# An FFN stage of two batches pulled ahead of its second half, and three more transposes given to the DMA

## The chip, the cores and the metric

The kernel runs on one core of a Trainium2 chip. The metric is the time of one execution on the device in microseconds (us). A run counts as slow when it is more than 1.5% above the fastest run of the same kernel; comparisons use the fast runs alone. A wait of TensorE is given as the profile has it, as the idle time ahead of a product.

## The reference

Eight batches of 448 tokens go through attention with a squared ReLU in place of the softmax (12 heads of width 64), and its output goes through one feed-forward block (768 to 3072 to 768) with a layer norm without offset ahead of it.

```python
scores = scale * np.matmul(q, k.transpose(0, 1, 3, 2))      # 8 x 12 x 448 x 448
attn = np.maximum(scores, 0.0) ** 2 / S
x = np.matmul(attn, v)                                      # then 8 x 448 x 768
# ...
xn = (x - mu) / np.sqrt(var + 1e-06) * g_ln
ch = np.maximum(xn @ w_ch1, 0.0) @ w_ch2
return (x + ch).astype(np.float32)
```

## The kernel before: the parts that matter

Heads are handled in pairs, six pairs to a batch: pairs 0 to 5 are batch 0, 6 to 11 batch 1, 12 to 17 batch 2. Attention of batch 0 runs by itself (to 28 us). From then on TensorE works in three layers. FFN1 of a batch makes 24 tiles of the hidden layer `h`. Between those tiles stand bursts ("excursions") of three tiles of attention scores, for the next batch. FFN2 follows: two tiles of batch 0 with plain products (`ffn_2_first`), everything else two tiles at a time with seven half-size products instead of eight (`seven`), for which VectorE makes sums of quarters of the second weight, `w2`, and of `h`.

All of the loads from memory that concern us are issued by GpSimd, one after another, in the order of the program. The transposes of `x_tok` (the residual by token) and of q and k are DMA transposes issued by SyncE. Pairs 0 to 11 get their q and k transposed on TensorE; pairs from 12 on by a DMA transpose out of a ring of three places.

```python
PE_T = 2                                   # batches whose q/k are transposed on TensorE

def att_T(i, copy=None, bank=None):
    if i >= PE_T * NPAIR:                  # pairs from 12 on
        new_qkT(i)
        nc.sync.dma_start_transpose(qkT[i], qk_ring[:, i % 3].rearrange("p j c -> p (j c)"))
        return
    # ... 16 transposes on TensorE and a copy out of PSUM

def load_qk(i):
    # ... q, k and the last keys of one pair of heads into the ring: three loads by GpSimd
    nc.gpsimd.dma_start(q_to, q[b, heads].rearrange("x (p j) d -> p j x d", j=NJ))
    nc.gpsimd.dma_start(k_to[:, :NF], k[b, heads, :SF].rearrange("x (p t) d -> p t x d", t=NF))
    nc.gpsimd.dma_start(k_to[:SS, NF], k[b, 2 * a:2 * a + 2, SF:].rearrange("x s d -> s x d"))

def w2_sums(slot, a, b, op, part):
    r = slice(part * KH // 2, (part + 1) * KH // 2)
    nc.vector.tensor_tensor(w2[:, slot, r], w2[:, a, r], w2[:, b, r], op=op)

IN_FIRST = (5, 8, 11, 14, 17, 20)          # FFN1 tiles of batch 0 followed by a burst
T_IN_FIRST = {10: 3, 13: 4, 16: 5}         # pairs 9, 10, 11 transposed on TensorE after these tiles
X_AT = (9, 10, 11, 12, 13, 14)             # DMA transposes of x_tok
STATS_AT = {0: (18, 21, 23), ...}          # layer norm statistics on VectorE

# ... the main sequence
        load_heads(1, [("q", 0, 2), ("k", 0, 2), ("k last", 0, H)])
        load_heads(1, [("q", 2, 4), ("k", 2, 4)])
        load_w1(0)
        load_w1(1)
        load_w1(2)
        load_heads(1, [("q", 6, 6), ("k", 6, 6), ("v", 0, H), ("v last", 0, H)])
        for c in range(3, NCH):
            load_w1(c)
        # ... attention of batch 0
        load_w2(B11, 0, 0)
        load_w2(B21, 1, 0)
        load_w2(B12, 0, 1)
        load_w2(B22, 1, 1)
        nc.gpsimd.memset(qk_ring, 0.0)
        i = PE_T * NPAIR
        load_qk(i)
        load_qk(i + 1)
        load_qk(i + 2)
        load_v(i)
        for b in range(B):
            ffn_1_all(b)
            if b == 0:
                ffn_2_first()              # two tiles of batch 0, plain
            else:
                ffn_2_all(b)               # the rest, seven products for two tiles
```

Of the kernel before, what the change touches and what calls it, by code (L numbers as in the profile page):

```python
# [11 lines left out]
def kernel(  # L12
# [93 lines left out]
    nc.vector.memset(v1_sb[:, H * NF * D:], 0.0)  # L106

# [18 lines left out]
    PE_T = 2  # L126
    EARLY = H * NJ * D
# [113 lines left out]
    def q_of(i, r):  # L241
        if i < PE_T * NPAIR:
            return by_j(flat(i)[r, :S])
        return qkT[i][r, :NJ, :SP]

    def k_of(i, r, t, keys):
        c0 = (S if i < PE_T * NPAIR else NJ * P) + t * P
        return flat(i)[r, c0:c0 + keys]

    def att_T(i, copy=None, bank=None):  # L250
        if i >= PE_T * NPAIR:
            new_qkT(i)
            nc.sync.dma_start_transpose(qkT[i], qk_ring[:, i % 3].rearrange("p j c -> p (j c)"))
            return
        new_qkT(i)
        if i == 0:
            for t, cp, n in ((0, nc.vector.tensor_copy, S), (1, nc.scalar.copy, SF)):
                ps = bf_view(next_f())
                pe_T(0, t, ps, range(NJ - t))
                cp(flat(0)[:, t * S:t * S + n], ps[:, :n])  # L260
            return
        if bank is None:
            bank = next_f() if i <= NPAIR else next_spare()
        ps = bf_view(bank)
        pe_T(i, 0, ps)
        pe_T(i, 1, ps, range(NJ - (i == 1)), S)
        n = S + (SF if i == 1 else S)
        (copy or nc.vector.tensor_copy)(flat(i)[:, :n], ps[:, :n])  # L268
# [108 lines left out]
    def gain(b, ki):  # L377
        nc.scalar.activation(xc[:, ki, :], xT_of(b, ki), Act.Identity, scale=g_sb[:, ki:ki + 1])

    def center(b):  # L380

        mean_ps = spare[1][:, :S]

        def parts(k0, k1):
            for ki in range(k0, k1):
                center_part(ki, mean_ps)

        def first():
            for c in range(2):
                nc.tensor.matmul(mean_ps[c * D:(c + 1) * D, :], ones[:, :D], xs, start=True, stop=True)  # L390
            parts(0, 2)

        return [first, lambda: parts(2, 4), lambda: parts(4, 6)]

    def center_part(ki, mean_ps):
        nc.vector.scalar_tensor_tensor(xc[:, ki, :], mean_ps, g_sb[:, ki:ki + 1], xc[:, ki, :],  # L396
# [16 lines left out]
    def ffn_rstd(b):  # L413
        ts = tiles_of(b)
        r = rstd[:, ts[0]:ts[-1] + 1]
        nc.scalar.activation(r, mv_sb[:, ts[0]:ts[-1] + 1, 1], Act.Sqrt, bias=eps_sb)
# [8 lines left out]
    def ffn_1(ni, bank=None):  # L425
        ps = (next_f() if bank is None else bank)[:, :S]
        for ki in range(K1):
            for c in range(2):
                n0 = ni * P + c * D
                nc.tensor.matmul(ps[c * D:(c + 1) * D, :], w1[:, ki, n0:n0 + D], xc[:, ki, :],  # L430
                                 start=(ki == 0), stop=(ki == K1 - 1))
        nc.scalar.activation(h[:, ni, CARRY:], ps, Act.Relu)  # L432

    def h_cols(b, m):
        c0 = CARRY + m * P - b * S
# [34 lines left out]
    held_stores = []  # L470

    def plain_part(b, m, dh, part, parts, box):
        if part == 0:
            box[m] = next_f()[:, :HD]
        n = K2 // parts
        cols = h_cols(b, m)
        for ki in range(part * n, (part + 1) * n):
            slot = ((B11, B12), (B21, B22))[ki // KH][dh]
            for c in range(2):
                t0 = cols.start + c * D  # L480
                nc.tensor.matmul(box[m][c * D:(c + 1) * D, :], h[:, ki, t0:t0 + D],  # L481
                                 w2[:, slot, ki % KH, :], start=(ki == 0), stop=(ki == K2 - 1))
        if part == parts - 1:
            o_t = new_acc() if dh else new_o()
            scaled_plus(o_t, box[m], m, x_half(m, dh))
            held_stores.append(lambda: store(o_t, m, dh * HD, (dh + 1) * HD))
# [21 lines left out]

    def seven(b, pair, banks, last, between):

        m1, m2 = 2 * pair, 2 * pair + 1
        a11, a12 = (h[:, r, h_cols(b, m1)] for r in (slice(0, KH), slice(KH, K2)))
        a21, a22 = (h[:, r, h_cols(b, m2)] for r in (slice(0, KH), slice(KH, K2)))
# [95 lines left out]
    def queued(i):  # L609
        if PE_T * NPAIR <= i + 3 < NP_ALL:  # L610
# [100 lines left out]
    def ffn_1_first():  # L711
        f_ps, m_ps = next_f(), next_f()
        tiles = [t[:, :S] for t in (f_ps, m_ps, spare[1], next_sc()[:, 0])]
        for ki in range(K1):
            if ki < GAIN_FIRST:
                center_part(ki, mean0)
# [3 lines left out]
            for ni, ps in enumerate(tiles):  # L720
                nc.tensor.matmul(ps, w1[:, ki, ni * P:(ni + 1) * P], xc[:, ki, :],  # L721
                                 start=(ki == 0), stop=(ki == K1 - 1))
        for ni, ps in enumerate(tiles):
            nc.scalar.activation(h[:, ni, CARRY:], ps, Act.Relu)
        for t in range(2):
            att_square(NPAIR, t)
        excursion(1)
# [3 lines left out]
    IN_FIRST = (5, 8, 11, 14, 17, 20)  # L731
    T_IN_FIRST = {10: 3, 13: 4, 16: 5}
    X_AT = (9, 10, 11, 12, 13, 14)
    V_AT = {21: PE_T * NPAIR + 2, 23: PE_T * NPAIR + 4}
    STATS_AT = {0: (18, 21, 23), 1: (10, 16, 19, 22), 2: (2, 5, 8, 14)}
    IN_SECOND = (3, 6, 9, 13, 15, 18, 21)
    IN_REST = (1, 4, 7, 10, 13, 16, 19)

    def ffn_1_all(b):
        ms = tiles_of(b)  # L740
        for ni in range(NI0 if b == 0 else 0, K2):
            if b == 0 and ni == NI0:
                ffn_1_first()
            if b == 0 and ni == X_AT[0]:

                nc.sync.dma_start(held, h[:1, ni - 1, CARRY:CARRY + 16])
            if b == 0 and ni in X_AT:
                ffn_x(b, X_AT.index(ni))
            if b == 0 and ni in V_AT:
                load_v(V_AT[ni])  # L750
            bursts = (IN_FIRST, IN_SECOND, IN_REST)[min(b, 2)]
            ffn_1(ni, spare[1] if b < B - 1 and ni in bursts and len(ready) > 1 else None)
            flush()
            at = STATS_AT[min(b, 2)][:len(ms)]
            if ni in at:
                ffn_stats(ms[at.index(ni)])
            if b == 1 and ni in SUMS_AT:
                w2_sums(*LATE_SUMS[SUMS_AT.index(ni)])
            if b == 0:
                if ni in IN_FIRST:  # L760
                    excursion(3)
                if ni == IN_FIRST[-1] + 3:
                    next_AV(bank=spare[1])
                if ni in T_IN_FIRST:
                    att_T(NPAIR + T_IN_FIRST[ni])
            elif b < B - 1:
                if ni in bursts:
                    excursion(3, **(dict(third=(nc.scalar, nc.vector), evac_by=nc.scalar) if b == 1 else {}))
                    while ni > bursts[1] and held_stores:
                        held_stores.pop(0)()  # L770
                if ni == min(bursts[-1] + 3, K2 - 1):
                    flush_loads()
                    next_AV(bank=spare[1])

    CENTER_AT = (4, 6, 8)
    SUMS_AT = (0, 1, 2, 4, 7, 11)
    LATE_SUMS = [(o, x, y, op, part)
                 for o, x, y, op in ((B_BOT, B21, B22, Alu.add), (B12, B12, B22, Alu.subtract),
                                     (B21, B21, B11, Alu.subtract)) for part in range(2)]
    def ffn_2_first():  # L780
        b = 0
        ffn_rstd(b)
        box = {}
        assert not ready
        steps = center(1)
        n = 0
        for dh in range(2):

            order = [(m, part) for m in range(2) for part in range(4)]
            if dh:  # L790
                order.sort(key=lambda x: x[1] // 2)
            for m, part in order:
                plain_part(b, m, dh, part, 4, box)
                if n < K1 - 1:
                    gain(1, n)
                if n == 3:
                    gain(1, K1 - 1)
                if n in CENTER_AT:
                    steps[CENTER_AT.index(n)]()
                if n == 2:  # L800
                    for ki in range(K1):
                        ffn_x(1, ki)
                if n == 8:
                    carry(b)
                if n in (9, 10):
                    w2_sums(B_TOP, B11, B12, Alu.add, n - 9)
                if n in (13, 15):
                    w2_sums(B_SUM, B11, B22, Alu.add, (n - 13) // 2)
                n += 1

    def ffn_2_all(b):
        ffn_rstd(b)
        x_bank, y_bank = f_turn.items
        z_bank = spare[0]
        first = b * S // (2 * P)
        pairs = range(first, (b + 1) * S // (2 * P))
# [7 lines left out]
        def between(n):  # L824
            n += 7 * (pr - first)
            if n == (8 if len(pairs) == 2 else 1):
                carry(b)
                if b < B - 1:
# [14 lines left out]
    with tc.manual_schedule(engines=set(ENGINES)):  # L843
# [3 lines left out]
        load_heads(1, [("q", 0, 2), ("k", 0, 2), ("k last", 0, H)])  # L847
        load_heads(1, [("q", 2, 4), ("k", 2, 4)])
        load_w1(0)
        load_w1(1)  # L850
        load_w1(2)
        load_heads(1, [("q", 6, 6), ("k", 6, 6), ("v", 0, H), ("v last", 0, H)])
# [8 lines left out]
        load_w2(B11, 0, 0)  # L861
        load_w2(B21, 1, 0)
        load_w2(B12, 0, 1)
        load_w2(B22, 1, 1)
        nc.gpsimd.memset(qk_ring, 0.0)
        i = PE_T * NPAIR
        load_qk(i)
        load_qk(i + 1)
        load_qk(i + 2)
        load_v(i)  # L870
        for b in range(B):
            ffn_1_all(b)
            if b == 0:
                ffn_2_first()
            else:
# [32 lines left out]
```

## Time and profile before

| | before |
|---|---|
| time, median of the first 3 runs | 520.9 us (519.87 to 521.59) |
| profiled span, granted clock | 518.9 us, 0.999 |
| TensorE busy | 511.8 us, 99% |
| VectorE, ScalarE, GpSimd busy | 71%, 53%, 43% |

Parts 1 and 2 of the profile's page. In part 2 the span is cut in 40 slices of 13 us; a digit is the busy share in tenths, PEclk the TensorE clock that was granted, and the row DMA the mean busy share of the 16 DMA engines.

```profile
span 518.9 us, 13591 instructions
...
PE 511.8 (99%) x5689; PEld 306.5 (59%) x5689; DVE 370.4 (71%) x658; ACT 276.8 (53%) x456; POOL 222.6 (43%) x255
...
PE   8999999999999999999999999999999999999996
...
PEclk9999999999999999999999999999999999999999
DMA  9999999999446992469934699269934300240022
GB/s 137 192 196 201 186 203 162 161 177 104 79 105 91 117 88 72 113 79 117 88 72 101 79 122 141 66 82 115 87 71 100 62 1 2 75 113 1 1 59 65
```

TensorE is at nine tenths or more in every slice but the ends, and the clock never drops. The DMA engines are at nine tenths or more in the first ten slices: they bring in the weights and the first inputs there. So TensorE sets the time, and the DMA engines have little slack before about 130 us.

The list of what TensorE waited for (engine and line, what it waited for, then us in total, times, longest us):

```profile
PE f L599 <- DVE w L103: 1.2, 1, 1.2
PE sc L288 <- DMA qkT_t<-qk_ring: 0.8, 1, 0.8
PE f L229 <- DMA w<-in_k_dram: 0.4, 1, 0.4
```

The whole kernel has 2.6 us of such waits. The chain of work that ended last, by engine, says the same:

```profile
PE 91%; DVE 3%; DMA 2%; ACT 2%; POOL 0%; issue 0%; POOLq 0%; ACTq 0%
```

The next lines are TensorE's timeline around 45 to 51 us: start, duration, line, product, and in square brackets (where there is one) the idle time ahead and what ended it. L430 is FFN1 and L229 the sixteen TensorE transposes of one pair.

```profile
46.27 0.76 PE L323 MATMUL f<-at,s_sb 128*64 128x448 bf16 x6
46.87 2.44 PE L430 MATMUL f<-xc,w 128*64 128x448 bf16 x24
49.14 0.68 PE L229 MATMUL f<-identity,w 112*64 112x112 bf16 x16
49.75 1.33 PE L430 MATMUL f<-xc,w 128*64 128x448 bf16 x12
51.01 0.55 PE L293 MATMUL sc<-qkT_t 64*128 64x448 bf16 x4
```

No line here has a bracket: FFN1 goes from tile to tile, and a pair's transposes add 0.61 us (from the start of L229 to that of the next line). The load of w1's fourth chunk, which tile 12 is the first to need, landed at 43.85. GpSimd's timeline has the issue of that load:

```profile
33.48 0.87 POOL L202 DMA_DIRECT2D w<-in_moe_w_ch_dram  x1 [3.39 <-DMA w<-in_moe_w_ch_dram]
```

The DMA engines of the same kernel from 36 to 56 us, in 40 slices of 0.5 us:

```profile
DMA  9999999999999999999999999999999999959999
GB/s 194 191 188 166 180 188 234 191 199 207 219 199 211 203 207 211 205 205 200 197 195 193 196 196 198 201 188 200 193 199 196 219 180 167 55 81 186 194 191 188
```

They keep close to 200 GB/s until about 52 us.

### The profile page before, as it was taken

To read this page: it belongs to the slowest core of one execution; us is meant where nothing else is said; L and a number is where in the kernel's file an instruction comes from. 1 tells how busy PE (TensorE), PEld (TensorE's weight loads), DVE (VectorE), ACT (ScalarE), POOL (GpSimd) and SP (SyncE) were. 2 spreads that over 40 slices of the span, in tenths; PEclk is the share of its full clock that TensorE was granted. 3 is DMA by queue.
4 is the path that set the end of the run, shared out by engine and by line. 5 is a ranking of instruction groups with operands and counts; after the bars stand their busy time and mean duration, and the time that the engine had idled before them with its cause. 6 is when DMAs were issued, how large, how long until landed. Compare 5 with 4: busy or idle time off the path is not lost.

```text
span 518.9 us, 13591 instructions
## 1 busy us (share of the span) xinstructions
PE 511.8 (99%) x5689; PEld 306.5 (59%) x5689; DVE 370.4 (71%) x658; ACT 276.8 (53%) x456; POOL 222.6 (43%) x255
## 2 busy tenths in 40 slices
PE   8999999999999999999999999999999999999996
PEld 4455566546765566655666556555665556665665
DVE  5966879778958669587685868787695866950255
ACT  6986633776247652476524765476524765234320
POOL 8727115778423853238532376247532000320031
PEclk9999999999999999999999999999999999999999
DMA  9999999999446992469934699269934300240022
GB/s 137 192 196 201 186 203 162 161 177 104 79 105 91 117 88 72 113 79 117 88 72 101 79 122 141 66 82 115 87 71 100 62 1 2 75 113 1 1 59 65
DMA packets 175245, 53.01 MB, mean 102 GB/s; under 512 B 154192, under 2 KB 175184, under 8 KB 175184
## 3 DMA queue, kind: packets, MB, share of 16 engines
q0 software_dynamic: 103680, 25.75, 53.0%
q1 hardware_dynamic: 70976, 26.03, 27.0%
q8 instruction: 44, 0.72, 0.6%
q10 hardware_dynamic: 528, 0.37, 0.2%
q14 instruction: 17, 0.14, 0.1%
HBM read 51.91 MB, written 11.01 MB: 121 GB/s over the span
## 4 chain that ended last, share of the span: by engine, by line
PE 91%; DVE 3%; DMA 2%; ACT 2%; POOL 0%; issue 0%; POOLq 0%; ACTq 0%
PE f L430 40%; PE f L498 34%; PE f L323 5%; PE sc L293 4%; PE f L481 3%; PE f L293 2%; DVE at L306 1%; ACT at L303 1%; DMA qkT_t<-qk_ring 1%; PE sc L288 1%; DMA w<-in_k_dram 1%; PE f L346 1%; PE f L721 1%; DVE xT L362 1%; DVE qkT_t L268 0%; ACT h L432 0%
## 5 line engine op out<-in xcount | busy, mean ns | idle before, releaser
L430 PE MATMUL f<-xc,w 128*64 128x448 bf16 x2256 | 225.5, 353 | 0.1
L430 PEld LDWEIGHTS <-w 128*64 128x64 bf16 x2256 | 125.9, 110 | 91.6 <-issue 13.6
L432 ACT ACTIVATE h<-f 128x448 bf16<-128x448 f32 x188 | 102.8, 547 | 102.5 <-PE f L430 97.6
L498 PE MATMUL f<-w,s_sb 128*64 128x384 bf16 (+2 forms) x1584 | 130.0, 324 | 0.0
L498 PEld LDWEIGHTS <-s_sb 128*64 128x64 bf16 x1584 | 90.0, 110 | 37.2
L303 ACT ACTIVATE at<-sc 128x896 bf16<-128x896 f32 x120 | 102.8, 918 | 5.1 <-PE sc L293 4.2
L306 DVE TENSOR_TENSOR at<-at 128x896 bf16<-128x896 bf16 x168 | 95.6, 618 | 4.9 <-ACT at L303 4.7
L531 POOL TENSOR_TENSOR o_t<-o_t,x_tok 128x384 f32<-128x384 f32 x26 | 24.4, 938 | 148.7 <-ACT o_t L530 148.7
L169 POOL DMA_DIRECT2D qk_ring<-in_q_dram x36 | 46.7, 1298 | 87.3 <-DMA qkT_t<-qk_ring 61.7
L299 DVE TENSOR_SCALAR at<-f 128x448 bf16<-128x448 f32 x89 | 52.7, 619 | 30.7 <-PE f L293 30.7
L530 ACT ACTIVATE o_t<-f,rstd 128x384 f32<-128x384 f32 x26 | 15.1, 582 | 93.5 <-issue 30.9
L492 DVE TENSOR_TENSOR s_sb<-h 128x1536 bf16<-128x1536 bf16 x65 | 64.1, 1002 | 0.0
L170 POOL DMA_DIRECT2D qk_ring<-in_k_dram x36 | 55.8, 1549 | 10.7 <-DMA w<-in_moe_w_ch_dram 10.7
L498 PE MATMUL f<-w,h 128*64 128x384 bf16 x624 | 52.9, 326 | 0.0
L171 POOL DMA_DIRECT2D qk_ring<-in_k_dram x36 | 46.8, 1300 | 5.1 <-DMA w<-in_moe_w_ch_dram 4.9
L498 PEld LDWEIGHTS <-h 128*64 128x64 bf16 x624 | 35.7, 110 | 15.3
L531 POOL TENSOR_TENSOR acc_t<-acc_t,x_tok 128x384 f32<-128x384 f32 x24 | 28.9, 1211 | 22.3 <-ACT acc_t L530 19.6
L323 PE MATMUL f<-at,v_ring 128*64 128x448 bf16 x288 | 35.7, 356 | 0.0
L181 POOL DMA_DIRECT2D v_ring<-in_v_dram x36 | 33.2, 1232 | 1.1 <-DMA qk_ring<-in_q_dram 1.1
L396 DVE SCALAR_TENSOR_TENSOR xc<-f,g_sb,xc 128x448 bf16<-128x448 f32 x45 | 28.5, 678 | 4.6 <-PE f L390 4.6
L362 DVE TENSOR_SCALAR xT<-f 128x448 bf16<-128x448 f32 x33 | 20.3, 617 | 15.5 <-PE f L323 12.5
L293 PE MATMUL sc<-qkT_t 64*128 64x448 bf16 x192 | 30.0, 356 | 0.1
(86 smaller groups left out, 391.0 us busy)
## 6 DMA issues: line engine op xcount, KB each, us to landing
w<-in_moe_w_ch_dram POOLq DMA_DIRECT2D x6, 768.0 KB, 12.9
w<-in_moe_w_ch_dram POOLq DMA_DIRECT2D x4, 1152.0 KB, 29.1
v_ring<-in_v_dram POOLq DMA_DIRECT2D x21, 192.0 KB, 4.9
qk_ring<-in_q_dram POOLq DMA_DIRECT2D x36, 112.0 KB, 5.2
qk_ring<-in_k_dram POOLq DMA_DIRECT2D x36, 96.0 KB, 5.3
out_dram<-o_t SPq DMA_DIRECT2D x8, 168.0 KB, 2.2
out_dram<-acc_t SPq DMA_DIRECT2D x7, 168.0 KB, 2.2
out_dram<-o_t SPq DMA_DIRECT2D x8, 144.0 KB, 2.1
```

The source lines that it names most:

```text
L170: nc.gpsimd.dma_start(k_to[:, :NF], k[b, heads, :SF].rearrange("x (p t) d -> p t x d", t=NF))
L171: nc.gpsimd.dma_start(k_to[:SS, NF], k[b, 2 * a:2 * a + 2, SF:].rearrange("x s d -> s x d"))
L293: nc.tensor.matmul(by_j(half[hh]), k_of(i, r, t, P), q_of(i, r), start=True, stop=True)
L299: nc.vector.tensor_scalar(at[:, x], half[x], 0.0, None, op0=Alu.max)
L303: nc.scalar.activation(at, ps[:, :, :S], Act.Relu)
L306: nc.vector.tensor_mul(attn[i, t], attn[i, t], attn[i, t])
L323: nc.tensor.matmul(ps[hh * D:(hh + 1) * D, :], weights, values, start=start, stop=stop)
L430: nc.tensor.matmul(ps[c * D:(c + 1) * D, :], w1[:, ki, n0:n0 + D], xc[:, ki, :], start=(ki == 0), stop=(ki == K1 - 1))
L432: nc.scalar.activation(h[:, ni, CARRY:], ps, Act.Relu)
L492: nc.vector.tensor_tensor(s_sb[:, n], x, y, op=op)
L498: nc.tensor.matmul(ps[c * D:(c + 1) * D, :d1 - d0], stat[:, ki, c * D:(c + 1) * D], w2[:, slot, ki, d0:d1], start=(start and ki == 0), sto ...
L531: nc.gpsimd.tensor_tensor(o_t, o_t, x_half(m, dh), op=Alu.add)
```

## The change

The change makes FFN1 of batches 0 and 1 one after the other, before any FFN2. w2 is then not needed until both are made, and its loads can keep out of the way of w1's. `h` has no room for all the tokens of two batches; the 256 tokens that are left over (tiles 5 and 6 of 128, in batch 1) lie in idle places, the rows of w2's unfinished sums and the scratch of the sums of `h`. w2's loads are issued later, at tile 22 of batch 0 and tile 5 of batch 1. The plain pair is now made of tiles 5 and 6, after FFN1 of batch 1. And pairs 9, 10 and 11 get q and k by DMA transpose, which spares TensorE 48 transposes but takes three more sets of small loads into the first 40 us. The sums of w2 move with its loads, four of them into FFN1 of batch 1.

```diff
+    nc.vector.memset(qk_ring, 0.0)
+    xc_1 = sums_flat[:, :K1 * S].rearrange("p (k s) -> p k s", k=K1)   # FFN1's input of batch 1
+    def h_extra(ki):                       # where the tokens of batch 1 lie that h has no room for
+        if ki < NXS:
+            return x_flat[:, ki * XP:(ki + 1) * XP]
+        # ...
+    DMA_T = NPAIR + 3
     def att_T(i, copy=None, bank=None):
-        if i >= PE_T * NPAIR:
+        if i >= DMA_T:
@@ FFN1's ReLU out of PSUM
+        elif b == 1:
+            nc.scalar.activation(h[:, ni, S:], ps[:, :HW - S], Act.Relu)
+            nc.scalar.activation(h_extra(ni), ps[:, HW - S:], Act.Relu)
@@ the places of things in FFN1
-    IN_FIRST = (5, 8, 11, 14, 17, 20)
-    T_IN_FIRST = {10: 3, 13: 4, 16: 5}
-    STATS_AT = {0: (18, 21, 23), 1: (10, 16, 19, 22), 2: (2, 5, 8, 14)}
+    BURSTS = {0: (5, 8, 11, 14, 17, 19), 1: (4, 7, 10, 13, 16, 19, 22), 2: (1, 4, 7, 10, 13, 16, 19)}
+    STATS_AT = {0: {18: 0, 21: 1, 23: 2}, 1: {8: 5, 11: 6}, 2: {11: 7, 14: 8, 17: 9}}
+    W2_AT = {(0, 22): ((B11, 0, 0), (B12, 0, 1)), (1, 5): ((B22, 1, 1), (B21, 1, 0))}
+    SUMS_AT = {15: (B_TOP, B11, B12, Alu.add, 0), 17: (B_TOP, B11, B12, Alu.add, 1),
+               20: (B_BOT, B21, B22, Alu.add, 0), 21: (B_BOT, B21, B22, Alu.add, 1)}
@@ the main sequence
-        load_heads(1, [("q", 0, 2), ("k", 0, 2), ("k last", 0, H)])
-        load_heads(1, [("q", 2, 4), ("k", 2, 4)])
+        load_heads(1, [("q", 0, 6), ("k", 0, 6), ("k last", 0, 6)])
         load_w1(0)
         load_w1(1)
+        load_qk(DMA_T)
         load_w1(2)
-        load_heads(1, [("q", 6, 6), ("k", 6, 6), ("v", 0, H), ("v last", 0, H)])
+        load_heads(1, [("v", 0, H), ("v last", 0, H)])
+        load_qk(DMA_T + 1)
+        load_qk(DMA_T + 2)
         for c in range(3, NCH):
             load_w1(c)
         # ...
-        load_w2(B11, 0, 0)
-        # ... the other three, the ring's clearing and q/k of pairs 12 to 14
-        load_v(i)
+        load_v(PE_T * NPAIR)
         for b in range(B):
             ffn_1_all(b)
-            if b == 0:
-                ffn_2_first()
-            else:
+            if b == 1:
+                ffn_2_beside()             # tiles 5 and 6, plain
+            if b > 0:
                 ffn_2_all(b)
```

## The prediction

> **What bounds the kernel.** The page's first part has TensorE busy 511.8 of 518.9 us (99%), and the chain of waits is 91% TensorE lines; the list of waits names only 2.6 us of TensorE waiting. Only fewer TensorE instructions, or fewer stretches below its pace, can pay.
>
> **TensorE work.** The order of instructions shows the same products in both kernels (24 full-width FFN1 products, now made for batch 1 too, take 188 ns each against two half-width ones of about 95: no gain). Only the transposes of pairs 9, 10 and 11 go: 48 instructions, 0.61 us a pair in the timeline, **-1.8 us**.
>
> **Pace.** FFN1 of batch 1 took 39.2 us (81.7 to 120.9 after TensorE's start), that of batch 2 37.35. The excess of 1.9 us is a 1.2 us wait for a q/k DMA transpose (7.2 us in the chain of waits, 105.5 to 112.7) and half-width products at 98 to 105 ns instead of 95. The change moves w2's loads later and returns ReLU work to VectorE: **up to -1.9 us**. With nothing else: 517.2.
>
> **What it costs.** The DMA engines are over 90% busy in the first nine slices (0 to 117 us). The change puts more on them before 62 us: q/k of pairs 9 to 11 as 128-byte packets (1.8 us a pair with the queue alone, 79.0 to 80.8) in place of two large loads (3.1 us for all three), and three transposes of eight tiles. The Trainium skill ("DMA: Bandwidth & Descriptors", Queues, rings and completion order) says each DMA engine alternates between queues packet by packet; the trace agrees: x_tok transposes landed 2.7 to 3.5 us apart beside w1's loads, 1.8 to 2.2 beside w2's. So a q/k transpose beside w1 is an estimated 7 us (64 packets against 24), plus 4.5 us of latency.
> My estimates: w1's fourth chunk lands at 46 to 48 us (before: 43.9), needed at 46.5; pair 10's transpose at 52, needed at 50.5; pair 11's at 61, needed at 60; the last x_tok transpose, behind both in one queue, at 61 to 64 (before: 60.7). The statistics of x_tok stand on VectorE ahead of the last burst's ReLUs and squares, so VectorE stalls, and through it TensorE. In batch 1, x_tok's transposes and those of pairs 15 and 16 meet w2's loads. Together **+1 to +7 us**; I take +2.3, not trusting the queue arithmetic to better than 2 us.
> ScalarE's second ReLU per FFN1 tile of batch 1 (an estimated +0.15 us on 0.55) fits in its idle time. The ring's clearing on VectorE (estimated 1.5 us, by 0.38 us for 384 words) ends before its first input lands (3.7): no cost.
>
> **Predicted: 519.5 us, 8 in 10 between 515.5 and 525.5.** Faster by over 2%: 0.03; within 2%: 0.93; slower by over 2%: 0.04.
>
> **What would show it.** Right: 48 fewer TensorE transposes; FFN1 of batch 1 at 37.5 to 38 us plus any transpose wait; FFN2 unchanged at 13.65 us a pair; TensorE waiting for w1, q/k transposes or (through VectorE's statistics) squares within 46 to 72 us; from batch 3 on timelines identical but for a shift. Wrong: no such waits in FFN1 of batch 0 and a time near 517; or waits of 3 us or more in FFN1 of batch 1.
>
> **What would make it wrong.** If transposes beside w1 get a better share than I think, all lands in time: 517. If the statistics hold VectorE until 64 us or later, the stage loses 5 to 7 us and the change is a loss of about 1%. A late w2 (last load at an estimated 104 us, needed for sums at 100) could stall VectorE in batch 1 too.

## The result, and the profile after

| | before | after |
|---|---|---|
| time, median of 4 runs | 520.6 us (519.87 to 521.59) | 538.15 us (537.12 to 542.02) |
| ratio, 95% interval | | 1.035 (1.0295 to 1.0404) |
| profiled span, granted clock | 518.9 us, 0.999 | 536.7 us, 0.99 |
| TensorE busy | 511.8 us | 517.3 us |
| matmul instructions | 5689 | 5617 |

A ratio is the mean time of one kernel's fast runs over that of the other's fast runs in the same rounds, so it is not quite the ratio of the medians. The change is slower by 3.5%: the prediction of 519.5 us, with 525.5 as its upper end, was wrong.

Parts 1 and 2 of the page of the changed kernel (slices of 13.4 us):

```profile
span 536.7 us, 13472 instructions
...
PE 517.3 (96%) x5617; PEld 308.7 (58%) x5617; DVE 371.4 (69%) x663; ACT 275.0 (51%) x473; POOL 227.6 (42%) x259
...
PE   8996989879999999999999999999999999999996
...
PEclk9998999989999999999999999999999999999999
DMA  9999999999723699359975399949954310250022
GB/s 137 192 177 158 165 152 175 187 178 144 80 61 75 101 120 85 81 118 91 114 52 94 90 113 124 92 81 114 92 66 105 69 21 4 57 121 1 1 53 68
```

TensorE has 72 instructions fewer (48 transposes, and 24 because 24 full-width products stand for 48 half-width ones), and yet it is busy for longer and idle for much longer: 19.4 us of the span against 7.1. The PE row dips in slices 4, 6, 8 and 9, and PEclk dips in slices 4 and 9. From slice 10 on the row is full.

What TensorE waited for:

```profile
PE sc L307 <- DMA qkT_t<-qk_ring: 5.1, 4, 2.2
PE f L448 <- DMA w<-in_moe_w_ch_dram: 4.4, 1, 4.4
...
PE f L506 <- DVE xT L381: 0.9, 1, 0.9
```

The first two lines are new in kind: 5.1 us for DMA transposes of q and k, and one wait of 4.4 us in FFN1 for a piece of w1. The chain that ended last shows how much of it went back through loads:

```profile
PE 72%; DMA 17%; POOL 4%; DVE 4%; issue 2%; ACT 0%; POOLq 0%; DVEq 0%; SPq 0%
```

17% of the chain is now DMA, where it was 2%. TensorE's timeline at the places that answer to those shown of before, and at one further wait:

```profile
45.78 0.76 PE L342 MATMUL f<-at,s_sb 128*64 128x448 bf16 x6
50.98 6.14 PE L448 MATMUL f<-xc,w 128*64 128x448 bf16 x36 [4.45 <-DMA w<-in_moe_w_ch_dram]
57.05 0.55 PE L312 MATMUL sc<-qkT_t 64*128 64x448 bf16 x4
...
57.73 3.60 PE L448 MATMUL f<-xc,w 128*64 128x448 bf16 x36
...
63.43 0.38 PE L307 MATMUL sc<-qkT_t 64*64 64x448 bf16 x2 [1.04 <-DMA qkT_t<-qk_ring]
...
98.62 0.38 PE L307 MATMUL sc<-qkT_t 64*64 64x448 bf16 x2 [1.56 <-DMA qkT_t<-qk_ring]
...
111.00 0.58 PE L307 MATMUL sc<-qkT_t 64*64 64x448 bf16 x2 [2.16 <-DMA qkT_t<-qk_ring]
```

Tile 12 of FFN1 comes at 50.98 us after 4.45 us without work, and the 36 products from there take 6.14 us, where the 36 from 57.73 take 3.60. That is the clock: the trace shows 0.5 granted from 49.4 to 56.2 us (6.8 us), and again from 110.8 to 114.2 (3.4 us), after the wait for pair 17's transpose. Before had no such stretch between the ends. The Trainium skill ("TensorE: Matmul & The Clock Gate", Part 1: The HAM clock gate) says that the array falls to half its rate after an idle window of about 3.4 us and needs a busy one to come back; the stretches agree, being 3.4 us, or two or three times that (3.4 and 6.8 here, 10.2 in e2 below). The length of the gap ahead of them does not always agree, as the last section says.

The DMA engines of the changed kernel from 36 to 56 us:

```profile
DMA  9999995789989999999999999499999999999999
GB/s 159 154 151 175 183 100 54 151 148 74 126 57 117 183 147 171 197 195 178 156 188 175 157 169 151 39 138 190 175 197 196 194 198 198 196 198 190 195 203 195
```

In the same 20 us they do not keep to 200 GB/s; in some half microseconds they fall to 54, 74 and 57 GB/s, and the window's mean is 160 GB/s against 190. The DMA row is still mostly nines. A digit 9 says only that packets were under way on the engines, not that bytes were moving well. The trace's packets from 37 to 38 us are 1064 of 128 bytes (133 KB) and 104 of a transpose, of 256 bytes (26 KB); from 31 to 32 us they were 197 of 1024 bytes (197 KB). That small packets are slower is stated by the Trainium skill ("DMA: Bandwidth & Descriptors", Why small descriptors are slow: a fixed overhead for each packet), and these numbers agree. But behind the lowest figures here stands something else, which the times of issue show (below, at e7): there was too little in the queue.

The timeline of both kernels can be cut into stages at the first product of each:

| stage, us | before | after | order alone (e1b) | DMA transposes alone (e2) | order alone, no w2 loads (e6) |
|---|---|---|---|---|---|
| attention of batch 0, ends at | 28.10 | 28.23 | 27.92 | 27.39 | 28.52 |
| FFN1 of batch 0 | 39.00 | 48.60 | 41.95 | 48.27 | 41.95 |
| plain pair | 15.79 | 16.93 | 18.04 | 18.23 | 16.93 |
| FFN1 of batch 1 | 39.20 | 44.15 | 45.05 | 42.12 | 37.65 |
| seven products, batch 1 | 27.49 | 28.54 | 28.53 | 27.49 | 28.54 |
| FFN1 of batch 2 | 37.34 | 38.06 | 37.77 | 37.34 | 37.88 |
| seven products of batch 2 begin at | 186.93 | 204.51 | 199.24 | 200.84 | 191.48 |

(The plain pair stands between the two FFN1 stages in before and in e2, and behind both in the others.) After that point the stages are the same to 0.01 us. So the whole loss, 17.6 us in the trace, lies before 205 us: 9.6 in FFN1 of batch 0, 4.95 in that of batch 1, 1.1 in the plain pair (of which 0.76 is a group of attention products that moved into it), 1.05 in the seven products and 0.7 in FFN1 of batch 2.

### The profile page after: what moved, and what is told of

Its sections match the earlier page's. It is cut to its first block, busy times and chain, and to the rows that moved or that the text cites. A ratio compares the mean times of both kernels' runs of the same rounds, so it can differ in the third digit from the quotient of the medians.

```text
span 536.7 us, 13472 instructions
## 1 busy us (share of the span) xinstructions
PE 517.3 (96%) x5617; PEld 308.7 (58%) x5617; DVE 371.4 (69%) x663; ACT 275.0 (51%) x473; POOL 227.6 (42%) x259
## 4 chain that ended last, share of the span: by engine, by line
PE 72%; DMA 17%; POOL 4%; DVE 4%; issue 2%; ACT 0%; POOLq 0%; DVEq 0%; SPq 0%
PE f L448 31%; PE f L523 31%; DMA w<-in_moe_w_ch_dram 6%; DMA qk_ring<-in_k_dram 4%; PE f L342 4%; DMA s_sb<-in_v_dram 3%; PE sc L312 3%; PE f L506 2%; DMA w<-in_k_dram 1%; DMA qkT_t<-qk_ring 1%; PE f L312 1%; DMA v_ring<-in_v_dram 1%; POOL qk_ring L188 1%; DVE w L230 1%; DVE s_sb L517 1%
## 5 line engine op out<-in xcount | busy, mean ns | idle before, releaser
L448 PE MATMUL f<-xc,w 128*64 128x448 bf16 x1968 | 198.7, 356 | 4.4 <-DMA w<-in_moe_w_ch_dram 4.4
L448 PEld LDWEIGHTS <-w 128*64 128x64 bf16 x2208 | 123.9, 111 | 97.2 <-issue 16.7
L459 ACT ACTIVATE h<-f 128x448 bf16<-128x448 f32 x144 | 78.6, 546 | 73.5 <-PE f L448 70.0
L318 DVE TENSOR_SCALAR at<-f 128x448 bf16<-128x448 f32 x96 | 56.6, 619 | 53.3 <-PE f L312 53.3
L188 POOL DMA_DIRECT2D qk_ring<-in_q_dram x39 | 51.2, 1312 | 99.0 <-DMA qkT_t<-qk_ring 76.8
L189 POOL DMA_DIRECT2D qk_ring<-in_k_dram x39 | 60.8, 1558 | 4.2 <-DMA w<-in_moe_w_ch_dram 4.2
L190 POOL DMA_DIRECT2D qk_ring<-in_k_dram x39 | 48.3, 1238 | 7.2 <-DMA w<-in_moe_w_ch_dram 5.7
L565 POOL TENSOR_TENSOR acc_t<-acc_t,x_tok 128x384 f32<-128x384 f32 x24 | 30.6, 1283 | 22.3 <-ACT acc_t L564 21.5
L200 POOL DMA_DIRECT2D v_ring<-in_v_dram x36 | 32.5, 1208 | 5.0 <-DMA w<-in_moe_w_ch_dram 4.7
L381 DVE TENSOR_SCALAR xT<-f 128x448 bf16<-128x448 f32 x34 | 21.0, 618 | 11.9 <-PE f L342 10.8
L196 POOL DMA_DIRECT2D v_ring<-in_v_dram x18 | 24.9, 1381 | 5.5 <-PE sc L312 5.5
## 6 DMA issues: line engine op xcount, KB each, us to landing
qk_ring<-in_q_dram POOLq DMA_DIRECT2D x39, 112.0 KB, 5.3
```

Source lines behind the costliest of these rows:

```text
L318: nc.vector.tensor_scalar(at[:, x], half[x], 0.0, None, op0=Alu.max)
L448: nc.tensor.matmul(ps[c * D:(c + 1) * D, :], w1[:, ki, n0:n0 + D], xc_of(b)[:, ki, :], start=(ki == 0), stop=(ki == K1 - 1))
L459: nc.scalar.activation(h[:, ni, CARRY:], ps, Act.Relu)
L565: nc.gpsimd.tensor_tensor(o_t, o_t, x_half(m, dh), op=Alu.add)
```

## The experiments

Two theories at the start. The first (DMA; theory A in the expectations) held that the three extra sets of small loads and the DMA transposes overload the DMA engines before 62 us, and that the order of the stages costs nothing. The rival (order; theory B) held that the new order itself costs: later w2, sums and statistics of VectorE in FFN1. Kernels are named by their edit; a diff is against the changed kernel unless it says otherwise.

### Each part alone

**e1_order_alone**: the changed kernel, with pairs 9 to 11 back on TensorE and the early loads as before.

```diff
-    DMA_T = NPAIR + 3
+    DMA_T = PE_T * NPAIR
+    T_IN_FIRST = {10: 3, 13: 4, 16: 5}
+                if ni in T_IN_FIRST:
+                    att_T(NPAIR + T_IN_FIRST[ni])
-        load_heads(1, [("q", 0, 6), ("k", 0, 6), ("k last", 0, 6)])
+        load_heads(1, [("q", 0, 2), ("k", 0, 2), ("k last", 0, H)])
+        load_heads(1, [("q", 2, 4), ("k", 2, 4)])
...
+        for i in range(3):
+            load_qk(DMA_T + i)            # after w1, before attention of batch 0
```

> The change without its DMA part: FFN1 of both batches ahead of FFN2, but pairs 9 to 11 transposed on TensorE again and their q/k loaded by the two large loads of before. Theory A (the DMA engines were overloaded before 62 us: w1's fourth chunk late, TensorE idle, clock halved, w2 late): FFN1 of batch 0 back to 39 us (48.6 in the change), no stretch at half clock, FFN1 of batch 1 at 38 to 41, total 519 to 524. Theory B (the new order itself costs: two ReLUs per FFN1 tile on ScalarE, sums of w2 crowded on VectorE behind the plain pair): FFN1 of batch 1 stays near 44 us and FFN2 of batch 1 near 28.5, total 526 or more.

Measured: ratio 1.025 (1.0201 to 1.0298), fast runs from 531.4 to 536.6 us.

**e2_dma_transposes_alone**: the kernel before, with only the DMA part of the change.

```diff
# against the kernel before
+    DMA_T = NPAIR + 3                     # used by att_T, q_of, k_of, queued
-                if ni in T_IN_FIRST:
-                    att_T(NPAIR + T_IN_FIRST[ni])
         load_w1(1)
+        load_qk(DMA_T)
         load_w1(2)
-        load_heads(1, [("q", 6, 6), ("k", 6, 6), ("v", 0, H), ("v last", 0, H)])
+        load_heads(1, [("v", 0, H), ("v last", 0, H)])
+        load_qk(DMA_T + 1)
+        load_qk(DMA_T + 2)
```

> The kernel before with only the DMA part: pairs 9 to 11 by DMA transpose, the loads in the order of the change. Theory A: FFN1 of batch 0 takes 47 to 49 us, with TensorE idle for about 4.5 us before w1's fourth chunk and a stretch at half clock; since w2 stands behind w1 and is needed right after, FFN2 of batch 0 may wait as well: total 529 to 536. Theory B: about 519, the three transposes saved.

Measured: 534.5 us, ratio 1.0268 (1.0239 to 1.0298). Its waits of TensorE (here L433 is FFN1 and L484 the plain FFN2):

```profile
PE f L433 <- DMA w<-in_moe_w_ch_dram: 7.6, 1, 7.6
PE sc L291 <- DMA qkT_t<-qk_ring: 2.2, 1, 2.2
PE f L484 <- DMA w<-in_moe_w_ch_dram: 2.1, 2, 1.5
```

The fourth piece of w1 landed at 53.2 us and TensorE waited 7.6 us for it, with half clock for 10.2 us; later it waited for w2's pieces, which stand behind w1 in the queue. FFN1 of batch 0 takes 48.27 us, as in the change.

So either part alone costs more than 2%: 12 us for the order, 13.7 for the transposes. Neither theory had it alone. The two do not add up to the 17.5 of the change. By the table, what the change loses falls short of the two losses added by 2.6 us in FFN1 of batch 0, 3.6 in the plain pair and 3.8 in FFN1 of batch 1. That a product which waits for two late things waits once would explain it, but no run tests that.

### Why w1's fourth piece is late

**e3_idle_filled**: 72 products of ones are put ahead of tile 12, into the time in which TensorE stood idle. If the half clock is a cost by itself, this saves it.

```diff
+            if b == 0 and ni == 12:
+                for _ in range(72):
+                    nc.tensor.matmul(spare[0][:, :P], ones, ones, start=True, stop=True)
```

> The change with 72 idle products (128 columns, about 55 ns each, 4 us in all) put before the FFN1 tile that waits for w1's fourth chunk, so that TensorE is not idle. If the slow products after the wait (36 in 6.1 us instead of 3.4) are the halved clock, they take 3.4 to 3.6 us, the stretch at half clock near 50 us is gone, and the total is 2 to 3 us less, 535 to 536. If they were slow for another reason (operands, evictions), they stay at 6 us and the total at 538.

Measured: 541.9 us, ratio 1.0408 (1.0379 to 1.0437); a miss. The half-clock stretch at 49 us was gone, as intended, but two new ones of 3.4 us came at 63.0 and 100.5, with longer waits for transposes (2.82 us at 63.4 and 2.28 at 100.5, where the change waited 1.04 and 1.56). FFN1 of batch 0 took 50.3 us, more than the 48.6 of the change. TensorE came to the product that needs pair 11's transpose 1.75 us sooner than in the change, and still went on at 63.4 us as there, because the transpose landed at 63.40 (63.38 in the change). So the half clock is not what the change loses there: what it saves, the next landing takes.

**e4_x_tok_late**: the transposes of x_tok of batch 0 go to tiles 18 to 23, out of the way of w1, and their statistics to batch 1.

```diff
-    X_AT = (9, 10, 11, 12, 13, 14)
+    X_AT = (18, 19, 20, 21, 22, 23)
-    STATS_AT = {0: {18: 0, 21: 1, 23: 2}, 1: {8: 5, 11: 6}, ...
+    STATS_AT = {0: {K2: 0}, 1: {8: 5, 11: 6, 14: 0, 17: 1, 18: 2}, ...
```

> The change with the six x_tok transposes of batch 0 at FFN1 tiles 18 to 23 instead of 9 to 14, and their statistics in batch 1. Theory A: 144 packets per DMA engine less beside w1: w1's fourth chunk at about 50 us (50.9), the fifth and sixth 1 to 2 us sooner, pair 11's transpose at 56 to 58 instead of 63.4, FFN1 of batch 0 3 to 5 us shorter; part is given back in batch 1, where they meet w2: total 533 to 537. If contention between queues does not matter, no change.

Measured: 540.7 us, ratio 1.0378 (1.0358 to 1.0398). w1's fourth piece landed at 50.93 us, exactly where it did in the change (50.94): the x_tok transposes do not delay it. They do delay pair 11's transpose, which now landed at 57.29 (63.38 in the change). FFN1 of batch 0 fell to 45.8 us, but that of batch 1 rose to 49.7, with one gap of 7.00 us that ended at 98.9, in which TensorE waited for VectorE. The gain was given back, and the expected 533 to 537 us was missed.

**e7_loads_no_transposes**: the small loads of pairs 9 to 11 stay, and there is no DMA transpose of them; TensorE transposes the data of pairs 6 to 8 again in their place. Its output is wrong, which doesn't matter for the time.

```diff
-    DMA_T = NPAIR + 3
+    DMA_T = PE_T * NPAIR
+                src = pr - 3 if b == 1 and pr > 2 else pr
-                                    sb[:rows, 2 * pr + hh, j], identity[:rows, :rows])
+                                    sb[:rows, 2 * src + hh, j], identity[:rows, :rows])
```

> The change with its loads of pairs 9 to 11 in small packets, but without their DMA transposes; TensorE transposes pairs 6 to 8 again in their place (a wrong result on purpose). If the small-packet loads and their issue delay w1's fourth chunk, it lands at 48 us or later with a wait of 2 us or more; if the transposes do, at 44 to 46 us with no wait.

Measured: 539.7 us, ratio 1.0372 (1.0351 to 1.0393). w1's fourth piece again landed at 50.92, and TensorE waited 4.00 us for it. The chain of waits of this kernel between 30 and 52 us shows the reason, piece by piece (start, us, what):

```profile
21.84 16.04 DMA s_sb<-in_v_dram
37.88 0.95 issue
38.84 1.15 POOL qk_ring L188
39.98 1.01 POOL qk_ring L189
...
41.08 9.84 DMA w<-in_moe_w_ch_dram
```

Read it upwards from the last line. w1's piece was issued only at 41.08 us and took 9.84 us to land. Ahead of its issue GpSimd issued q and k of pair 11 (L188 and L189), which it could not do before the large load of v had landed, at 37.88. In the kernel before, w1's fourth piece was issued at 33.48 us and took 10.4 us; in the change it was issued at 40.63 and took 10.3. In these three kernels it takes about as long, but starts 7.1 us later. GpSimd's timeline of the change has the same order of events:

```profile
38.38 1.15 POOL L188 DMA_DIRECT2D qk_ring<-in_q_dram  x1 [3.19 <-DMA s_sb<-in_v_dram]
...
40.63 3.08 POOL L221 DMA_DIRECT2D w<-in_moe_w_ch_dram  x3
```

The semaphores in the trace show why: GpSimd's loads use eight of them in turn, and the n-th load is issued only once the (n-8)-th has landed. (Whether the chip or only this program's use of semaphores sets the number eight, no run shows.) Three q/k sets are nine loads instead of two large ones (pairs 6 to 8 need two loads fewer, three for five), v's last rows another four, and so the eight places were taken by small loads and by v, which stood behind w1's pieces and landed only 16 us after its issue. When v had landed, little was left under way: in the change the loads' queue moved 46, 2 and 44 KB in the microseconds from 38 to 41 us, where it moves some 190 to 200 with large packets when full.

**e8_transposes_no_loads**: the reverse. The three early sets of loads are taken out and the DMA transposes kept (they move zeros). Its output is wrong, which doesn't matter for the time.

```diff
-        load_qk(DMA_T)
-        load_qk(DMA_T + 1)
-        load_qk(DMA_T + 2)
```

> The complement: the three DMA transposes of the change, of a ring that is only cleared, without the small-packet loads of pairs 9 to 11 (a wrong result on purpose). If the loads are the cause, w1's fourth chunk lands at 42 to 44 us and nothing waits for it; if the transposes are, at 46 us or later. Pair 11's transpose still has x_tok transposes and w1 beside it, so a wait of 1 to 3 us for it may stay.

Measured: 532.3 us, ratio 1.023 (1.021 to 1.0251). w1's fourth piece landed at 41.18, so the loads alone made it late. But pair 9's transpose landed at 47.59 and TensorE waited 2.44 us for it. FFN1 of batch 0 took 45.1 us: both the loads (47.75 alone) and the transposes (45.08 alone) exceed the 41.95 of the order alone. (e8 has 48 TensorE transposes fewer than e7 and the order alone, 1.8 us.)

**e5_w1_fourth_first**: w1's fourth piece ahead of v in the order of loads.

```diff
         load_w1(2)
+        load_w1(3)
         load_heads(1, [("v", 0, H), ("v last", 0, H)])
...
-        for c in range(3, NCH):
+        for c in range(4, NCH):
```

> The change with one load moved: w1's fourth chunk ahead of v of batch 1 and of the q/k of pairs 10 and 11. If the order of the loads is the fault, the 4.5 us wait and the stretch at half clock go and the total falls by 5 us or more, to 533 or less. If it is the amount of work on the DMA engines, the chunk lands at about 41 to 43 us and that wait goes, but pair 10's and 11's transposes and the later chunks come later by as much, and the total falls by less than 3 us (535 to 539).

Measured: 539.1 us, ratio 1.036 (1.034 to 1.0381). The piece landed at 38.13, far ahead of need, but now pair 10's transpose landed at 56.38 and TensorE waited 5.86 us for it and then 1.46 for pair 11's, with 6.8 us of half clock. FFN1 of batch 0 took 49.4 us. The total did not fall.

**e9_small_loads_between**: the small loads are spread: q/k of pairs 9 and 10, w1's third piece, q/k of pair 11, v, w1's fourth piece, v's last rows.

```diff
         load_w1(1)
         load_qk(DMA_T)
-        load_w1(2)
-        load_heads(1, [("v", 0, H), ("v last", 0, H)])
         load_qk(DMA_T + 1)
+        load_w1(2)
         load_qk(DMA_T + 2)
-        for c in range(3, NCH):
+        load_heads(1, [("v", 0, H)])
+        load_w1(3)
+        load_heads(1, [("v last", 0, H)])
+        for c in range(4, NCH):
```

> The change with the same loads in another order: the small q/k loads of pairs 9 to 11 stand between w1's chunks (pair 9 and 10 before the third, pair 11 after it) and w1's fourth chunk before the four small loads of v, so that the eight loads that may be under way always hold large ones. If the software queue ran dry (48, 11 and 20 KB in the three microseconds from 38 us, against 190) because small loads filled the eight places, w1's fourth chunk lands at 44 to 46 us, the 4.5 us wait and the first half-clock stretch go, FFN1 of batch 0 takes 43 to 46 us (48.6) and the total is 532 to 536. If the amount of bytes and packets alone delayed it, it lands at 48 us or later.

Measured: 540.1 us, ratio 1.0369 (1.0349 to 1.0389). w1's fourth piece landed at 45.81, in time. (The 48, 11 and 20 KB of the expectation are those of e7's trace.) The queue of loads no longer ran dry: from 36 to 43 us it moved 146 to 197 KB in every microsecond, and from 36 to 56 us all the queues had a mean of 182 GB/s (160 in the change). The waits of TensorE:

```profile
PE sc L307 <- DMA qkT_t<-qk_ring: 6.9, 4, 2.8
PE f L365 <- DMA s_sb<-in_v_dram: 3.3, 4, 1.2
```

No line for w1 is left; instead there are four waits for v's last rows (which landed from 46.3 to 49.9 us) and more waiting for transposes than in the change. The first stretch at half clock did not go: it was 6.8 us, from 48.0. FFN1 of batch 0 took 51.5 us, so the expectation held for the landing and the queue and missed the stage and the total.

Three orders of the same loads gave 48.6, 49.4 and 51.5 us for this stage, each with the wait at another load. What is late is not one load: with three pairs more on the DMA engines, more has to land before 65 us than lands in time in any of the orders that were tried. Nor is the dry queue the loss: e9 filled it and was no faster. Issuing the small loads from another engine than GpSimd, so that they take none of the eight places, was not tried.

### What the order of the stages costs

**e6_order_alone_no_w2**: e1_order_alone, with w2 set by GpSimd to a constant instead of being loaded. It asks whether w2's loads, which now fall into FFN1 of batch 1, are the cost of the order. Its output is wrong, which doesn't matter for the time.

```diff
# on top of e1_order_alone
-        nc.gpsimd.dma_start(w2[:, slot], w2_view[:, kh * KH:(kh + 1) * KH, dh * HD:(dh + 1) * HD])
+        nc.gpsimd.memset(w2[:, slot], 0.01)
```

> The order alone (e1), with w2 set to a constant by GpSimd instead of loaded (a wrong result on purpose). If w2's loads beside the transposes of pairs 15 to 17 and the sums waiting for w2's last quarter are what e1 loses in batch 1, both waits on transposes (1.6 and 1.9 us) and the half-clock stretch near 107 us go, FFN1 of batch 1 takes about 37 us without its moved attention product, total 524 to 527. What remains is the tail of FFN1 of batch 0 (2.5 us, the chain of the last pair's products, mean and centring that the plain pair used to cover) and the sums on VectorE (1 to 2 us). If w2's loads are not the cause, batch 1 stays as in e1 (531 or more).

Measured: 525.5 us, ratio 1.0101 (1.0084 to 1.0118). FFN1 of batch 1 takes 37.65 us, which is what the prediction expected of it, and there is no half clock and no wait for a transpose beyond 0.2 us. So w2's loads cost the new order some 7 us, and it stays 5 us slower than before even without them. (In e6 GpSimd spends 17 us on setting w2; whether a part of the 5 us is that was not tested.)

**e1b_order_alone_again**: the same kernel as e1_order_alone.

> The kernel of e1 once more, because its profile fell into the slow state. Total 531 to 534; FFN1 of batch 0 about 41.5 to 42 us without any wait for w1, and the waits for the transposes of pairs 15 and 17 in batch 1 as in the slow profile, 1.5 to 2 us each.

Measured: 532.7 us, ratio 1.0227 (1.0207 to 1.0247), two runs. TensorE's waits:

```profile
PE f L506 <- DVE xT L381: 3.6, 1, 3.6
PE sc L307 <- DMA qkT_t<-qk_ring: 3.2, 2, 1.7
```

The longest is for VectorE (L381 copies an attention output out of PSUM). VectorE's own timeline says what held that copy up:

```profile
111.70 2.63 DVE L230 TENSOR_TENSOR w<-w 128x2304 bf16<-128x2304 bf16 x2 [3.21 <-DMA w<-in_moe_w_ch_dram]
114.25 0.62 DVE L381 TENSOR_SCALAR xT<-f 128x448 bf16<-128x448 f32 x1
```

VectorE had been idle for some 3.2 us until a piece of w2 landed (the trace has its last quarter at 111.51, issued at 80.43), because the next thing in its order was the sum of two quarters of w2. The copy stood behind it, and TensorE behind the copy, until 114.9. Then came 3.4 us at half clock. A wait on a DMA thus appears in TensorE's list as a wait for VectorE.

**e13_sums_after_w2**: on top of e1_order_alone, the sums that need w2's last quarters are taken out of FFN1 of batch 1 and put into the plain pair.

```diff
# on top of e1_order_alone
-    SUMS_AT = {15: (B_TOP, B11, B12, Alu.add, 0), 17: (B_TOP, B11, B12, Alu.add, 1),
-               20: (B_BOT, B21, B22, Alu.add, 0), 21: (B_BOT, B21, B22, Alu.add, 1)}
+    SUMS_AT = {15: (B_TOP, B11, B12, Alu.add, 0), 17: (B_TOP, B11, B12, Alu.add, 1)}
+                        if n in (8, 10):
+                            w2_sums(B_BOT, B21, B22, Alu.add, (n - 8) // 2)
```

> The order alone (e1), with the two sums of w2's lower half moved from FFN1 tiles 20 and 21 of batch 1 into the plain pair, so that VectorE no longer waits there for w2's last quarter (landed at 111.5 us, TensorE waited 3.6 us for a copy behind the sums and then ran at half clock for 3.4 us). If that is the larger part of the 7.2 us that w2's loads cost in e1, the wait and the half-clock stretch go and the total is 527 to 529 (532.7). If the transposes of pairs 15 and 17 beside w2 are the larger part, less than 2.5 us is gained.

Measured: 527.6 us, ratio 1.0131 (1.0111 to 1.0151). That is 5 us less than the order alone, in four runs within 0.6 us, and no half clock, as expected. So about 5 of the 7 us that w2's loads cost ran through VectorE's sums; for the rest there are the waits of attention products for q/k transposes beside w2's loads, 1.50 us at 91.4 and 1.15 at 98.0.

**e14_half_w2_early**: e13 with half of w2 (two quarters) loaded ahead, right after v of pair 12, and only the other half in batch 1.

```diff
# on top of e13_sums_after_w2
-    W2_AT = {(0, 22): ((B11, 0, 0), (B12, 0, 1)), (1, 5): ((B22, 1, 1), (B21, 1, 0))}
+    W2_AT = {(0, 22): ((B22, 1, 1), (B21, 1, 0))}
         load_v(PE_T * NPAIR)
+        load_w2(B11, 0, 0)
+        load_w2(B12, 0, 1)
```

> e13 with half of w2 loaded right behind w1 and batch 2's first q/k, and the other half where the change starts loading w2. If the place of w2's loads is at fault, the transposes of pairs 15 and 17 have less beside them: their waits (2.0 and 1.9 us) fall to under 1 us together, total 524 to 526, near e6 with no w2 at all (525.5). If it is only the amount of work for the DMA engines, the wait moves to the transposes of pairs 12 to 14 at the start of batch 1 and the total stays within 1 us of e13.

Measured: 531.5 us, ratio 1.0196 (1.0167 to 1.0225): 4 us worse than e13, so both expectations missed. VectorE's timeline:

```profile
85.20 0.56 DVE L439 BATCH_NORM_STATS2 stats<-x_tok 128x6 f32<-128x384 bf16 x1 [0.77 <-DMA x_tok<-xT]
91.79 0.56 DVE L440 BATCH_NORM_STATS2 stats<-x_tok 128x6 f32<-128x384 bf16 x1 [6.03 <-DMA x_tok<-xT]
...
92.51 1.10 DVE L318 TENSOR_SCALAR at<-f 128x448 bf16<-128x448 f32 x2
```

The early half of w2 now runs beside the x_tok transposes of batch 1; their last one landed at 91.67 us, where it landed at 77.91 in e13. VectorE's statistics waited 6.03 us for it, the ReLU of a burst (L318) stood behind them, and TensorE waited 5.44 us for that ReLU, with 6.8 us of half clock. Both places for w2 collide with something that VectorE needs in order.

**e10_no_w2_stats_moved**: e6, with the statistics of batch 0 moved into batch 1, to see whether they make the rest of the order's cost. Its output is wrong, which doesn't matter for the time.

```diff
# on top of e6_order_alone_no_w2
-    STATS_AT = {0: {18: 0, 21: 1, 23: 2}, 1: {8: 5, 11: 6}, ...
+    STATS_AT = {0: {K2: 0}, 1: {8: 5, 11: 6, 14: 0, 17: 1, 18: 2}, ...
```

> e6 (order alone, w2 not loaded, wrong on purpose) with the statistics of batch 0 moved from the tail of its FFN1 into that of batch 1. If VectorE's crowding at the tail is what FFN1 of batch 0 still loses in e6 (41.95 us against 39.0), it gets 1 to 2.5 us shorter and the total is 523 to 524.5 (525.5). If the chain of the last pair itself (squares, product, copy, sum, mean, centring) sets it, less than 0.7 us is gained.

Measured: 527.4 us, ratio 1.0128 (1.0111 to 1.0145). FFN1 of batch 0 fell by 1.17 us, to 40.78, and that of batch 1 rose by 3.17, to 40.82: VectorE has no free place there, and TensorE waited 1.8 us for one of its copies. The statistics explain about 1.2 of the 2.95 us that FFN1 of batch 0 is longer in e6 than before, but nothing is won by moving them.

### Was there anything to gain in FFN1 of batch 1?

**e12_before_stores_later**: the kernel before, with the held stores of FFN2 let go two bursts later, so that the q/k transpose that TensorE waited 1.2 us for is not held up by them.

```diff
# against the kernel before
-                    while ni > bursts[1] and held_stores:
+                    while ni > bursts[3] and held_stores:
```

> The kernel before with the stores of the plain pair let go from the fifth burst on instead of the third, since they stand on SyncE's queue and the DMA engines just ahead of the transpose that TensorE waited 1.2 us for. If that wait is theirs, it goes and the total falls by up to 1.2 us, to 519.2 to 520 (a gain below the scatter of single runs); otherwise 520.4.

Measured: 520.65 us against 520.76, ratio 0.9997 (0.9985 to 1.0009). The wait is gone and FFN1 of batch 1 takes 38.13 us instead of 39.20. (That wait is the 0.8 us of the list of before; from the start of the product ahead of it, it is 1.2.) But the plain pair took 16.46 instead of 15.79, with a wait of 0.51 us at 79.84 for the last piece of w2, which landed at 79.80 (78.96 in before). The plain pair lies ahead of the first store that the edit moves, so this is not the edit's doing but the difference of one execution from another. Why the medians of 6 and 11 runs show no gain all the same stays open.

## Why the prediction was wrong, point by point

- **What bounds the kernel** was right: TensorE, 99% busy, and only fewer instructions or fewer stalls could pay.
- **Fewer transposes, -1.8 us**: right in the count, 48 fewer. They are worth 1.8 us at 0.61 us a pair, and the loss had to be made in spite of them.
- **Pace of FFN1 of batch 1, up to -1.9 us**: the number came out without w2's loads (37.65 us in e6, "37.5 to 38" in the prediction), in part by luck: of the 1.55 us by which e6 is below the 39.20 of before, 0.76 is the group of attention products that moved into the plain pair, so the pace itself gained some 0.8 us. With w2's loads it was not to be had: 44.15 us in the change. The prediction moved w2's loads later and counted that as help for this stage; they are what fell into it.
- **The step that failed is "Together +1 to +7 us; I take +2.3".** The trace lost 17.6 us, and 1.8 us of transposes were saved besides, so this term measured about 19 us (21 if the pace is counted as gained, as in the predicted 517.2 us). It was too small in three ways:
  - *The landing times were estimated from shares of the queue, as if every load were waiting in it.* The prediction had w1's fourth piece at 46 to 48 us. It landed at 50.94, because it was issued 7.1 us later than before. The loads that may be under way at a time are counted, eight, not weighed; replacing two large loads by nine small ones delayed the issue of what follows. This is shown by e7 (late without any of the transposes), e4 (late without x_tok beside it) and e5 and e9 (in time when issued earlier). But with this piece in time the stage was no shorter (49.4 us in e5, 51.5 in e9, 48.6 in the change): the lateness moved to the transposes and to v, so what was mis-sized is all that has to land before 65 us, and not this load alone. The pairs' transposes also came otherwise than predicted: pair 10's at 45.2 (52 predicted), pair 11's at 63.4 (61 predicted), the last x_tok at 66.6 (61 to 64).
  - *Lateness was costed as time past the need, and nothing else.* Two further items came with the idle time: the half clock (36 products in 6.14 us rather than 3.60, so 2.5 us at the first stretch), and, of the pairs of an even and an odd number, the last keys of both are multiplied with the even one, one burst ahead of where the prediction put the odd pair's need; the wait at 63.43 us is one of those. e3 shows that the half clock is no separate sum that could be won back: without it the next landing was waited for longer.
  - *The late w2 was named as a risk ("could stall VectorE in batch 1 too") and given no time.* It cost the order alone 7 us, 5 of them through sums that stand on VectorE ahead of copies that TensorE needs (e6, e13).
- **The order itself, with nothing late, costs 5 us** (e6), which the prediction had at zero. The trace has it in the end of FFN1 of batch 0 (2.95 us), in the plain pair (1.14, of which 0.76 moved there from FFN1 of batch 1), in the seven products of batch 1 (1.05), FFN1 of batch 2 (0.5) and the first stage (0.4), less the 1.55 us that FFN1 of batch 1 is shorter. e10 shows that 1.2 us of the first are VectorE's statistics. For the others I have an argument, not a run: the plain pair used to stand between the last attention products of batch 1 and its FFN1, and hid the chain from the last squares through their copy and the mean to the centred input; in the new order TensorE waits for that chain (0.33 us ahead of one of the last products and 0.57 at the mean, in the trace of e6).
- **The signs that were named** were mostly there: waits for w1 and for q/k transposes within 46 to 72 us, FFN1 and FFN2 from batch 3 on the same but for a shift. The waits through VectorE's statistics were not: x_tok landed at 66.6 us, later than the 64 us named as dangerous, and yet TensorE's waits for squares in FFN1 of batch 0 are 0.8 us in four pieces, as in e1b, where x_tok landed at 57.3. FFN2 was not unchanged either: the seven products of batch 1 took 28.54 us instead of 27.49. "Waits of 3 us or more in FFN1 of batch 1" was named as a sign of being wrong; the waits there were 1.56 and 2.16 us.
- **ScalarE's second ReLU fits** was right: the two ReLUs take about 0.34 and 0.39 us in the change instead of one of 0.55, and FFN1 of batch 1 runs at 37.65 us with them in e6. The clearing of the ring at the start cost nothing that shows: attention of batch 0 ends at 28.23 us against 28.10.

Left open: the two parts cost 12.0 and 13.7 us alone and 17.5 together; the overlap of 8 us lies in the stages named at e2, and what makes it was not tested. In the change w1's fourth piece moved at 76 to 177 KB per us from 45 to 50 us, with at most 34 KB of transposes beside it, where the two together reach about 190 afterwards; no run says why. None of the thirteen edits of either kernel that were tried beats the kernel before.

## What to carry to other kernels

Before moving work to the DMA engines, follow the issuing engine's list, not only the bytes: count how many loads may be under way, which slow one holds a place, and when the load that the next stage needs can be issued at all. Three orders of the same loads did no better than one another; if one wait goes, look where the next one comes, and try the order on the chip before trusting it. And where weights arrive late, keep whatever consumes them out of the in-order path of the engine that also empties the matmul banks.

## What the Trainium skill lacked or had wrong

- "DMA: Bandwidth & Descriptors": Queues, rings and completion order describes how queues share an engine (in turn, by packet), and the trace agrees where both queues have work: x_tok transposes landed 2.7 to 3.5 us apart beside w1 and 1.8 to 2.2 beside w2. It does not lead one to ask what is in the queue: here, in the change, the loads of GpSimd used eight semaphores in turn, the ninth load waited for the first, and a queue that moves 190 to 200 KB per us fell to 46, 2 and 44 KB in three successive microseconds. I found this limit stated on none of the pages that I used.
- "TensorE: Matmul & The Clock Gate", Part 1: the window of about 3.4 us agrees with the stretches seen (3.4, 6.8 and 10.2 us at half clock). The page's rule there, no idle gaps over about 3.4 us, is not strict enough here: gaps of 2.16 us (in the change, at 111.0) and 2.44 us (in e8, at 47.6) went with a stretch of 3.4 us at half clock, and three gaps of 1.24, 1.15 and 0.75 us between 45.1 and 49.2 us (in e9) with one of 6.8 us. Nor does the length of one gap decide: 2.21 us (in e5, at 112.0) and 2.76 us (in e3, at 122.7) had none. And e3 shows that filling the gap need not pay (541.9 us filled, 538.15 not).
- No page gives a size for how far a busy share of the DMA engines near 100% can go with less throughput: here 160 GB/s from 36 to 56 us in the change against 190 in the kernel before, at mostly nines in the profile's row in both.
